# Weight conversions in five stages, and the last stage's scales, loads and splits a batch ahead on ScalarE: attention and two mixers on one core

## The chip, the cores and the metric

One core of a Trainium2 chip runs the whole program. The metric is device microseconds of one execution. The engines are named as in the profile: PE (TensorE, matrix products; PEld is its weight loads), DVE (VectorE), ACT (ScalarE), POOL (GpSimd) and SP (SyncE, whose queue issues most DMAs). Each engine works through its own queue in order; between queues there are only semaphores.

## What is computed

Causal attention of 4 batches, 12 heads, 448 positions and 64 columns per head feeds two mixers, all in float32 by the reference:

```python
scores = scale * np.matmul(q, k.transpose(0, 1, 3, 2))      # mask, softmax, then times v
x = attn_out.transpose(0, 2, 1, 3).reshape(B, S, H * D)     # 4 x 448 x 768
# first mixer
h = np.maximum(xt @ w_tok1, 0.0) @ w_tok2                   # xt: x with positions last
u = x + h.transpose(0, 2, 1)
x = u + np.maximum(u @ w_ch1, 0.0) @ w_ch2                  # 768 -> 1536 -> 768
# second mixer
theta = x @ w_theta
y = einsum(w_tok_r, x * cos(theta)) + einsum(w_tok_i, x * sin(theta))
u = x + y
out = u + np.maximum(u @ w_ch, 0.0)
```

q, k and v come as float32, the weights as float64.

## The kernel before

**Numbers.** Most products run as three fp16 matmuls (`mm3`, lines 225 to 227). A float32 tile is scaled by a power of two and *split* into a high half and a rest (`split_to`, 191): the high half is a scaled copy on ACT (L157) or POOL (L160), the rest a subtraction on DVE (L193) that reads the high half. The scale comes from `power` (133): `squares` (120) lets ACT sum a tile's squares per row (L124) into a float32 column and POOL adds a tiny constant and writes bf16 (L125); PE adds the columns over the rows with a matrix of ones (L138), DVE cuts the sum to a power of two (L140, L128), and POOL makes scale and inverse from it (L131).

**Weight conversions.** Every float64 weight tile (768 KB) is fetched as raw words (L170), ACT takes the absolute value of the high words (L173), DVE puts low bits and sign right (L180 to L182), then come squares, power and split into a `ws` tile that is stored to DRAM (384 KB) and streamed in again for each use (L220). Four tiles of the token weights and 24 of `w_ch1` and `w_ch2` are converted beside the first half of attention; the table `ROUNDINGS` says at which attention step: `round_first` (511) does the absolute values there, `round_rest` (516) everything else one step later, and then issues the fetch of the tile after next. Seven of the 24 tiles are handed to their first unit without a reload. Six tiles of `w_ch` follow late (`convert_late`).

**Stages.** (1) Attention: 4 x 6 pairs of heads x 7 tiles = 168 steps. A step's scores (L329) go through DVE (row maximum, L336) and ACT (exponential, L338); PV (L373, L384) comes `LAG` = 4 steps later. After every two pairs `tokmix` (403) mixes tokens; when a batch's three mixings are done, `split_ready` (493) computes the power of u and splits its six tiles. (2) The first mixer's channel part runs as 96 *units* (24 a batch: 6 + 6 + 6 + 6 products of 18 matmuls), the first 72 spread over attention by `UNIT_STEPS`, the first of them at step 46. They end in `x2d` in DRAM. (3) Last stage, from about 655 us: theta weights `th` and token kernel `wk` have been loaded beside the last units; for each batch the x power, six x tiles loaded from `x2d` and split, on even batches also the `rawt` tails of two batches (split into `tl`), then two halves `dh` of: theta tiles (PE, then a chain through ACT, POOL and DVE to sine and cosine products, both split), `mix` over the token kernel, and after both halves `split_u2` (814) and six output units (736). The output units of a batch run in the next one: three after its first thetas, three at its end. All splits of this stage have their high half on POOL (`split`, 706).

**Order.** The program is traced by the Python code, and a scheduler then orders each engine's queue by its own timing of the instructions; `high_priority` pulls attention forward, and `issue_after` puts what is traced inside it behind a given instruction of the same engine. So the order that the chip sees isn't the order of the code.

Of the kernel before, what the change touches and what calls it, by code (L numbers as in the profile page):

```python
# [28 lines left out]
BUFS = dict(ut=12, h2=8, acc=12, ws=8, wf=2, raw=2, sb=3, ph=3, pt=5, t=3, junk=2)  # L29
# [3 lines left out]
KEEP, UBACK = 6, 16  # L33
LATE_CONVERT = 16
FIRST_UNIT, PHASE, RATES = 46, 42, (14, 29)
UNIT_STEPS = [FIRST_UNIT + -(-n * PHASE // RATES[0]) if n < RATES[0] else
              FIRST_UNIT + PHASE + -(-(n - RATES[0]) * PHASE // RATES[1]) for n in range(72)]
AHEAD_STEPS = {0: 18, 1: 22, 2: 26, 3: 30, 4: 34, 5: 38, 12: 43, 13: 47, 14: 51, 15: 55, 16: 70, 17: 77,
               18: 80, 19: 85, 20: 88, 21: 91, 22: 94}
ROUNDINGS = sorted([(at_step, n - 4) for n, at_step in enumerate((3, 4, 8, 9))] +  # L40
                   [(AHEAD_STEPS.get(n, UNIT_STEPS[n] - 5), n) for n in range(24)])
# [15 lines left out]
def fused(ctx, tc, q, k, v, w_tok1, w_tok2, w_ch1, w_ch2, w_theta, w_tok, w_ch, out):  # L57
# [46 lines left out]
    nc.vector.memset(ones, 1.0)  # L104
    trig_k = cst.tile([P, 4], F32, tag="trig_k", name="trig_k")
# [27 lines left out]
    def power(p, s, sq):  # L133

        ps = mm_bank()
        n = sq.shape[-1]
        for j in range(n):
            nc.tensor.matmul(ps[:, 0:1], lhsT=ones, rhs=sq[:, j:j + 1], start=j == 0, stop=j == n - 1)  # L138
# [56 lines left out]
    def split_scaled(dst, f, p):  # L195
        sq = main.tile([P, 1], BF16, tag="sqb", name="sqb", bufs=4)
        s = main.tile([P, 1], F32, tag="s", name="s", bufs=4)
        squares(sq, f)
        power(p, s, sq)
        split_to("A", dst, f, s)  # L200
# [9 lines left out]
    def convert(src, kept, p):  # L210

        w, f = ws_tile(), wf_tile()
        load64(f, src, raw_tile())
        split_scaled(w, f, p)
        nc.sync.dma_start(out=kept, in_=w)
        return w
# [86 lines left out]
    class Pair:  # L303
        def __init__(self, b, pr, parts):
# [4 lines left out]
            self.pts, self.ps = {}, None  # L309
            self.native_pv = b * NPR + pr in NATPV  # L310

    def scores(pp, i, h):
# [48 lines left out]
        nc.sync.dma_start_transpose(out=pt[:, 0:nb, :], in_=ph[:, 0:nb * P])  # L361
# [154 lines left out]
    def round_rest(j):  # L516
        n, f = ROUNDINGS[j][1], rounding.pop(j)
        round64(f, fetched.pop(j)[1])
        if n < 0:
            split_w(tok_weights(n + 4)[1], f)  # L520
        else:
            w, kept = ws_tile(), jobs[n][1]
            split_scaled(w, f, jobs[n][2])
            nc.sync.dma_start(out=kept, in_=w)
            stored.add(n)
            if n not in AHEAD_STEPS:
                loaded[n] = w
        fetch(j + 2)
# [3 lines left out]
    def convert_late(n):  # L532
        while made[0] < min(n, len(late)):
            with tc.issue_after(loads[min(LATE_CONVERT, max(loads))].ins):
                convert(*late[made[0]])
            made[0] += 1

    def run_units(n):
        for _ in range(n):
# [13 lines left out]
            split_ready()  # L553
# [12 lines left out]
    def mix_tokens():  # L566
        b, g = mixes.pop()
        tokmix(b, g, xgs[b, g], xbufs, accs[b])
        split_ready()
# [14 lines left out]

    for n, (b, pr, t) in enumerate(steps):
# [9 lines left out]
        for j, (at_step, _) in enumerate(ROUNDINGS):  # L595
            if at_step == n - 1:
                with tc.issue_after(pairs[b, pr].first.ins):
                    round_rest(j)
            if at_step == n:
                with tc.issue_after(pairs[b, pr].last.ins):  # L600
                    round_first(j)
        if n >= 140:
# [17 lines left out]
    with tc.issue_after(unit_end[0].ins):  # L620
        mix_tokens()
    convert_late(len(late))
# [37 lines left out]
    power(p_wk, s_wk, sq_wk)  # L660
    for t in range(7):
        split_to("A", wk[:, t], wkf[:, t], s_wk)
# [43 lines left out]
    def split(dst, src, s):  # L706
        split_to("P", dst, src, s)
# [48 lines left out]
    trigs = {}  # L756

    for b in range(B):
        for b2 in range(b, b + 2 if b % 2 == 0 else b):
            power(p_x[:, b2:b2 + 1], s_x[:, b2:b2 + 1], sq_x[b2])  # L760
            trigs[b2] = trig_table(b2)
        raw, x2 = [], []
        for d in range(DT):
# [5 lines left out]
            raw.append(r)  # L769
            x2.append(t)  # L770
        if b % 2 == 0:
            rawt = m2.tile([P, DT, P], F32, tag="rawt", name="rawt", bufs=1)
            for d in range(DT):
                for b2 in range(2):
                    nc.sync.dma_start(out=rawt[:, d, b2 * 64:(b2 + 1) * 64], in_=x2d[b + b2][d][:, 0:64])
            tl = m2.tile([P, 2, DT, P], F16, tag="tl", name="tl", bufs=1)
            for b2 in range(2):
                c = slice(b2 * 64, (b2 + 1) * 64)
                split(tl[:, :, :, c], rawt[:, :, c], s_x[:, b + b2:b + b2 + 1])
            tail_k = m2.tile([P, 9], F32, tag="tail_k", name="tail_k", bufs=1)  # L780
            for b2 in range(2):
                r = slice(b2 * 64, (b2 + 1) * 64)
                product(tail_k[r, 0:8], trigs[b + b2][r, 0:8], 1.0, 1.0)
        mix_scale = m2.tile([P, 1], F32, tag="mix_scale", name="mix_scale", bufs=2)
        product(mix_scale, p_x[:, b:b + 1], p_wk, 2.0 ** -28)
# [17 lines left out]

        def mix(dh):
            for d in range(3):
# [101 lines left out]
```

## Time and profile before

| | us |
|---|---|
| median of 3 runs | 996.02 (994.8 to 998.42) |
| the profiled execution, its own time | 993.12 |
| its span, first to last instruction | 991.3 |
| PE busy | 889.8 |
| DVE busy | 652.4 |
| ACT busy | 493.7 |
| POOL busy | 247.9 |
| mean granted TensorE clock | 0.954 of 2.4 GHz |

The profile is one execution. A group of instructions is named by line, engine and the tiles that it writes and reads. Idle time of an engine is put down to what ended it. A matmul that was issued while the one before still ran overlaps it, so busy time of PE is counted once.

### The profile page before, as it was taken

To read this page: it belongs to the slowest core of one execution; us is meant where nothing else is said; L and a number is where in the kernel's file an instruction comes from. 1 tells how busy PE (TensorE), PEld (TensorE's weight loads), DVE (VectorE), ACT (ScalarE), POOL (GpSimd) and SP (SyncE) were. 2 spreads that over 40 slices of the span, in tenths; PEclk is the share of its full clock that TensorE was granted. 3 is DMA by queue.
4 is the path that set the end of the run, shared out by engine and by line. 5 is a ranking of instruction groups with operands and counts; after the bars stand their busy time and mean duration, and the time that the engine had idled before them with its cause. 6 is when DMAs were issued, how large, how long until landed. Compare 5 with 4: busy or idle time off the path is not lost.

```text
span 991.3 us, 16726 instructions
## 1 busy us (share of the span) xinstructions
PE 889.8 (90%) x5935; PEld 570.0 (57%) x5935; DVE 652.4 (66%) x1498; ACT 493.7 (50%) x1155; POOL 247.9 (25%) x520
## 2 busy tenths in 40 slices
PE   7988699898877999998999989949999969989998
PEld 6877577666643656665656555525555535535554
DVE  6586677958897665747776258574678555674762
ACT  6687677867675554546554246432333312321521
POOL 2121012212311010111211112263445254343240
PEclk9999899989997999998999999979999988989999
DMA  6465553647979874846576678500441130203102
GB/s 191 126 212 172 193 189 134 227 157 211 253 200 259 254 214 130 212 128 134 181 153 174 207 243 273 186 32 9 141 123 51 54 104 15 97 9 129 52 26 75
DMA packets 104788, 146.93 MB, mean 148 GB/s; under 512 B 60992, under 2 KB 72192, under 8 KB 104704
## 3 DMA queue, kind: packets, MB, share of 16 engines
q1 hardware_dynamic: 104160, 144.84, 49.9%
q0 software_dynamic: 384, 0.79, 0.3%
q8 instruction: 47, 0.77, 0.3%
q14 instruction: 37, 0.30, 0.1%
q10 hardware_dynamic: 160, 0.23, 0.1%
HBM read 109.64 MB, written 22.81 MB: 134 GB/s over the span
## 4 chain that ended last, share of the span: by engine, by line
PE 64%; DMA 11%; DVE 10%; ACT 5%; POOL 5%; issue 4%; SPq 0%; ACTq 0%; DVEq 0%; POOLq 0%
PE ps_mm L225 14%; PE ps_mm L226 14%; PE ps_mm L227 14%; DMA pt<-ph 7%; PE ps_sc L329 3%; PE ps_pv L373 3%; PE ps_mm L345 2%; PE ps_sc L225 2%; PE ps_sc L226 2%; PE ps_sc L227 2%; POOL ut L160 2%; PE ps_pv L384 1%; PE ps_mm L410 1%; PE ps_mm L411 1%; PE ps_mm L409 1%
## 5 line engine op out<-in xcount | busy, mean ns | idle before, releaser
L225 PE MATMUL ps_mm<-h,ws 128*128 128x448 f16 x432 | 155.4, 361 | 0.0
L227 PE MATMUL ps_mm<-h,ws 128*128 128x448 f16 x432 | 155.2, 360 | 0.0
L226 PE MATMUL ps_mm<-h,ws 128*128 128x448 f16 x432 | 155.1, 361 | 0.0
L225 PEld LDWEIGHTS <-ws 128*128 128x128 f16 x720 | 71.6, 99 | 71.5 <-issue 14.2
L227 PEld LDWEIGHTS <-ws 128*128 128x128 f16 x720 | 71.5, 99 | 65.4 <-issue 6.4
L225 PE MATMUL ps_mm<-ut,ws 128*128 128x448 f16 x288 | 102.7, 359 | 6.2 <-ACT ut L157 6.2
L226 PEld LDWEIGHTS <-ws 128*128 128x128 f16 x720 | 71.4, 99 | 63.7 <-issue 6.1
L226 PE MATMUL ps_mm<-ut,ws 128*128 128x448 f16 x288 | 102.3, 356 | 0.0
L227 PE MATMUL ps_mm<-ut,ws 128*128 128x448 f16 x288 | 102.2, 355 | 0.0
L338 ACT ACTIVATE sb<-sb,mx 128x192 f32<-128x192 f32 (+3 forms) x168 | 89.0, 531 | 20.1 <-DVE mx L336 19.9
L336 DVE CUSTOM_DVE_ANT_0 sb<-ps_sc,mask 128x192 f32<-128x192 f32 (+3 forms) x168 | 74.3, 456 | 19.5 <-PE ps_mm L345 12.8
L124 ACT ACTIVATE junk<-acc 128x448 bf16<-128x448 f32 x72 | 41.1, 571 | 83.9 <-DVE acc L811 44.9
L373 PE MATMUL ps_pv<-v_raw,ptf 128*128 128x128 f32 (+1 forms) x456 | 62.4, 276 | 3.8 <-ACT ptf L347 2.4
L373 PEld LDWEIGHTS ps_pv<-v_raw,ptf 128*128 128x128 f32 x456 | 58.3, 191 | 9.0 <-ACT ptf L347 3.7
L457 ACT ACTIVATE t<-ps_mm,c_scale 128x448 f32<-128x448 f32 x48 | 30.1, 626 | 58.6 <-PE ps_mm L227 41.8
L160 POOL TENSOR_SCALAR h<-t 128x448 f16<-128x448 f32 x48 | 31.9, 664 | 105.8 <-ACT t L457 105.4
L329 PE MATMUL ps_sc<-kh,qs 128*128 128x256 f32 (+2 forms) x112 | 45.1, 411 | 13.4 <-DVE mx L336 10.8
L358 DVE SCALAR_TENSOR_TENSOR ph<-sb,ph 128x64 f16<-128x64 f32 (+3 forms) x156 | 42.8, 318 | 21.5 <-ACT ph L157 20.9
L459 DVE TENSOR_TENSOR h<-t,h 128x448 f16<-128x448 f32 x48 | 30.5, 640 | 39.3 <-POOL h L160 39.2
L157 ACT ACTIVATE ph<-sb 128x192 f16<-128x192 f32 (+3 forms) x84 | 36.4, 440 | 38.9 <-DMA pt<-ph 38.3
L698 ACT ACTIVATE tmp<-tmp 128x384 f32<-128x384 f32 x28 | 14.6, 523 | 76.7 <-DVE tmp L696 76.1
L225 PE MATMUL ps_sc<-th,ut 128*128 128x384 f16 x144 | 48.9, 340 | 3.2 <-POOL ut L160 1.8
(212 smaller groups left out, 2169.8 us busy)
## 6 DMA issues: line engine op xcount, KB each, us to landing
ws<-w_c SPq DMA_DIRECT2D x113, 384.0 KB, 4.1
raw<-in_w_ch_dram SPq DMA_DIRECT2D x30, 768.0 KB, 4.8
w_c<-ws SPq DMA_DIRECT2D x30, 384.0 KB, 3.4
q_raw<-in_q_dram SPq DMA_DIRECT2D x16, 448.0 KB, 4.5
k_raw<-in_k_dram SPq DMA_DIRECT2D x16, 448.0 KB, 4.4
v_raw<-in_v_dram SPq DMA_DIRECT2D x24, 288.0 KB, 3.9
x2d<-acc SPq DMA_DIRECT2D x24, 224.0 KB, 3.2
acc<-x2d SPq DMA_DIRECT2D x24, 224.0 KB, 2.8
```

The lines of the kernel that those rows point to most:

```text
L124: nc.scalar.activation(j[:, 0:src.shape[-1]], src, AF.Square, accum_out=a)
L157: nc.scalar.activation(dst, src, AF.Copy, scale=scale)
L160: e.tensor_scalar(out=dst, in0=src, scalar1=scale, scalar2=0.0, op0=ALU.mult, op1=ALU.add)
L225: nc.tensor.matmul(ps, lhsT=ka(a[:, 0]), rhs=kb(b[:, 0]), start=first, stop=False)
L226: nc.tensor.matmul(ps, lhsT=ka(a[:, 0]), rhs=kb(b[:, 1]), start=False, stop=False)
L227: return nc.tensor.matmul(ps, lhsT=ka(a[:, 1]), rhs=kb(b[:, 0]), start=False, stop=last)
L329: nc.tensor.matmul(ps[:, 0:n], lhsT=lhs, rhs=cut(pp.kh), start=True, stop=pp.kl is None)
L336: pp.first = nc.vector.tensor_tensor_reduce(out=dst, in0=src, in1=msk, op0=ALU.add, op1=ALU.min, scale=-0.125, scalar=3.0e38, accum_out=pp ...
L338: pp.last = nc.scalar.activation(sb[:, 0:kk], sb[:, 0:kk], AF.Exp, bias=pp.mx[:, j:j + 1], scale=-1.0, accum_out=pp.sm[:, j:j + 1])
L358: nc.vector.scalar_tensor_tensor(out=dst, in0=sb[:, c0:c1], scalar=PSC, in1=hi[:, c0:c1], op0=ALU.mult, op1=ALU.subtract)
L373: pp.pv = nc.tensor.matmul(pp.ps[:, reg:reg + n], lhsT=pt[:, u], rhs=pp.v[0][:, vt * D:vt * D + n], start=(u == 0), stop=(u == len(blks) - 1))
L459: gates[0] = nc.vector.tensor_tensor(out=t[:, 1], in0=f, in1=t[:, 0], op=ALU.subtract)
```

## The change

- `squares` writes ACT's accumulator straight into the bf16 column. The POOL addition is gone; `power` starts its sum with one matmul on a constant column `tiny` instead.
- The conversions run in stages: `round_first` (absolute values) at a step, `round_bits` (DVE's bits and ACT's squares) one later, the fetch of the tile after next two later, `round_split` (power, split with the high half on POOL) three later, `round_store` five later. `round_split` is traced in `late_step`'s place, behind the PV of the step four back; fetch and store stand behind the last transposing DMA of the pair on SP. `wf` has three buffers. The steps are evenly spaced from 14 to 92. No tile is handed over: all 24 are stored and reloaded.
- Units start at step 50 and reach the old rate at 88. `split_ready` runs two steps behind a batch's last mixing (steps 48, 90, 132); for the last batch one unit later than before.
- Last stage: `split` takes ACT. The x powers of batches 0 to 2 (`x_scale`) are traced in the units of the next batch, that of batch 3 between the two mixings of batch 0; the split of `wk` moves behind the first thetas. Loads and splits of x (`load_x2`) are traced a batch ahead, before the second mixing, the tails (`load_tail`) just before; three output units come after the second thetas in place of the batch's end (two, two and two in the last batch).

```diff
-BUFS = dict(..., wf=2, ...)
+BUFS = dict(..., wf=3, ...)
+ROUND_BITS, ROUND_FETCH, ROUND_SPLIT, ROUND_STORE = 1, 2, 3, 5
...
     def squares(dst, src):
-        a = main.tile([P, 1], F32, tag="sq", name="sq", bufs=4)
-        nc.scalar.activation(j[:, 0:src.shape[-1]], src, AF.Square, accum_out=a)
-        nc.gpsimd.tensor_scalar(out=dst, in0=a, scalar1=1.0, scalar2=TINY, op0=ALU.mult, op1=ALU.add)
+            nc.scalar.activation(j[:, 0:src.shape[-1]], src, AF.Square, accum_out=dst)
...
+        nc.tensor.matmul(ps[:, 0:1], lhsT=ones, rhs=tiny, start=True, stop=False)
...
-    def round_rest(j):
+    def round_bits(j):
         round64(f, fetched.pop(j)[1])
...
+            rounding[j] = f, row_squares(f)
+    def round_split(j):
+            f, sq = rounding.pop(j)
+            rounding[j] = ws_tile()
+            split_scaled("P", rounding[j], f, jobs[n][2], sq)
+    def round_store(j):
+            nc.sync.dma_start(out=jobs[n][1], in_=rounding.pop(j))
...
+            if at[0] % 24 == 2 and 1 <= at[0] // 24 <= 3:
+                x_scale(at[0] // 24 - 1)
...
+            with tc.issue_after(pairs[steps[n - LAG][0:2]].pv.ins):
+                for j, (at_step, _) in enumerate(ROUNDINGS):
+                    if at_step == n - ROUND_SPLIT:
+                        round_split(j)
+                if n in (b2 * 42 + 48 for b2 in range(B)):
+                    split_ready()
...
     def split(dst, src, s):
-        split_to("P", dst, src, s)
+        split_to("A", dst, src, s)
...
             thetas(0)
-            run(todo, 3)
+            run(todo, n)
             mix(0)
             thetas(1)
+            run(todo, n)
+            if b < B - 1:
+                if b == 1:
+                    load_tail(2)
+                load_x2(b + 1)
             mix(1)
             f = split_u2()
-            run(todo, 3)
+            run(todo, 6 - 2 * n)
```

How this moves instructions is shown at three places. Rows are engine queues in order, with the line numbers of each kernel's own file; behind `<-` stand the tiles read.

ACT, the first converted weight tile, before (`sq` is the float32 column, `ws` the split's high half) and then after (`sqb` is the bf16 column):

```order
L347 ACTIVATE ptf<-ps_mm 128x512
L338 ACTIVATE sb_182,sm<-sb_182,mx 128x192
L173 ACTIVATE wf<-raw 128x768
L124 ACTIVATE junk,sq<-acc 128x448 x2
L124 ACTIVATE junk,sq<-wf 128x768
L157 ACTIVATE ws<-wf,s 128x768
```

```order
L340 ACTIVATE sb_186,sm<-sb_186,mx 128x320
L173 ACTIVATE wf<-raw 128x768
L349 ACTIVATE ptf<-ps_mm 128x256
L124 ACTIVATE junk,sqb<-wf 128x768
L340 ACTIVATE sb_182,sm<-sb_182,mx 128x320
L349 ACTIVATE ptf<-ps_mm 128x256
```

The high half is gone from ACT's queue, and what follows the squares is attention's next work.

The start of the last stage: POOL before (`ut<-acc` are batch 0's x splits, `tl` the tails), then ACT after, where the first unit of batch 3 is evicted by the last row:

```order
L160 TENSOR_SCALAR h_8006<-t 128x448
L131 TENSOR_SCALAR s_x<-g 128x1
L131 TENSOR_SCALAR trig<-p_x,p_th 128x1
L131 TENSOR_SCALAR s_x<-g 128x1
L131 TENSOR_SCALAR mix_scale<-p_x,p_wk 128x1
L131 TENSOR_SCALAR trig<-p_x,p_th 128x1
L131 TENSOR_SCALAR mix_scale<-p_x,p_wk 128x1
L131 TENSOR_SCALAR trig<-s_x 128x1
L160 TENSOR_SCALAR ut<-acc,s_x 128x448 x3
```

```order
L157 ACTIVATE ut<-acc,s_u 128x448 x6
L157 ACTIVATE ut<-acc,s_x 128x448
L173 ACTIVATE thf<-raw_w 128x384
L157 ACTIVATE ut<-acc,s_x 128x448 x3
L124 ACTIVATE junk,sq_x_160<-acc 128x448
L124 ACTIVATE junk,sq_th<-thf 128x768
L173 ACTIVATE thf<-raw_w 128x384 x2
L124 ACTIVATE junk,sq_th<-thf 128x768
L157 ACTIVATE tl<-rawt,s_x 128x6x64 x2
L173 ACTIVATE thf<-raw_w 128x384
L157 ACTIVATE ut<-acc,s_x 128x448
L459 ACTIVATE t<-ps_mm,c_scale_145 128x448
```

Before, the x splits stand behind the last unit's split and a row of scales; after, they stand ahead of all units of batch 3.

PE at the start of batch 2, before (the end of the powers of x, the transposes, the first theta product on the tails `tl`) and after:

```order
L138 LDWEIGHTS ones
L138 MATMUL ps_mm<-sq_x_159,ones 128x1
L712 MATMUL ps_mm<-ident,rawt 128x128 x3
L712 MATMUL ps_mm<-ident,acc 128x128 x9
L225 LDWEIGHTS tl
L225 MATMUL ps_sc<-th,tl 128x384
```

```order
L138 LDWEIGHTS ones
L138 MATMUL ps_mm<-sq_y_163,ones 128x1
L740 MATMUL ps_mm<-ident,rawt 128x128 x2
L227 LDWEIGHTS tl
L227 MATMUL ps_sc<-th,tl 128x384
```

The twelve columns of x are gone from between the batches; what stands there now is the power of batch 1's own result (`sq_y`), with one transpose of the next tails inside it.

## Rows read from the trace of the kernel before

**Rows 1.** The page: the span, then PE's busy time.

```profile
span 991.3 us, 16726 instructions
PE 889.8 (90%) x5935; PEld 570.0 (57%) x5935; DVE 652.4 (66%) x1498; ACT 493.7 (50%) x1155; POOL 247.9 (25%) x520
```

**Rows 2.** Five stages: length, then busy us of each engine, granted clock, DMA.

```profile
0.00:250.00 250.00, 216.43 (x1423) 173.32 (x1423) 180.46 (x472) 181.56 (x444) 44.40 (x117) 0.95 0.56 182
250.00:330.00 80.00, 62.30 (x491) 41.51 (x491) 65.20 (x172) 49.31 (x117) 16.39 (x35) 0.87 0.95 250
330.00:580.00 250.00, 241.72 (x1975) 155.71 (x1974) 152.17 (x402) 124.87 (x309) 33.96 (x90) 0.99 0.67 172
580.00:655.00 75.00, 70.50 (x392) 36.75 (x391) 51.41 (x120) 38.83 (x85) 18.71 (x49) 0.98 0.68 219
655.00:991.30 336.30, 298.87 (x1662) 162.70 (x1660) 203.21 (x334) 99.18 (x204) 134.41 (x231) 0.95 0.20 65
```

**Rows 3.** PE's waits, whole span: us in total, times, longest us.

```profile
PE ps_sc L225 <- POOL tl L160: 21.2, 2, 12.5
PE ps_mm L138 <- POOL sqb L125: 15.1, 8, 4.2
...
PE ps_mm L225 <- ACT ut L157: 6.2, 2, 4.5
...
PE ps_mm L225 <- POOL ut L160: 4.5, 1, 4.5
PE ps_mm L138 <- POOL sq_u L125: 4.5, 3, 1.6
...
PE ps_mm L712 <- DVE g L140: 2.0, 1, 2.0
```

**Rows 4.** Timeline 43.5 to 48.5: start, us, instruction, count, idle before.

```profile
45.81 0.83 ACT L124 ACTIVATE junk<-wf 128x768 bf16<-128x768 f32 x1
...
46.81 0.19 POOL L125 TENSOR_SCALAR sqb<-sq 128x1 bf16<-128x1 f32 x1 [0.63 <-ACT junk L124]
47.05 0.16 PE L138 MATMUL ps_mm<-sqb,ones 128*128 128x1 bf16 x1 [2.20 <-POOL sqb L125]
```

**Rows 5.** Stretches of lower granted clock: columns as in rows 2.

```profile
47.00:51.00 4.00, 3.94 (x12) 2.58 (x12) 3.71 (x12) 3.09 (x9) 0.38 (x3) 0.57 0.00 0
...
197.00:205.00 8.00, 5.87 (x22) 3.29 (x21) 6.34 (x14) 5.29 (x12) 1.20 (x4) 0.57 0.84 282
...
658.00:672.00 14.00, 3.92 (x13) 1.91 (x14) 9.72 (x13) 0.63 (x2) 11.44 (x19) 0.51 0.00 0
812.00:826.00 14.00, 6.21 (x21) 3.03 (x22) 6.53 (x9) 0.00 (x0) 9.78 (x20) 0.51 0.13 47
873.00:880.00 7.00, 5.56 (x15) 2.04 (x16) 5.81 (x11) 2.09 (x4) 3.28 (x5) 0.53 0.00 0
```

**Rows 6.** Lines L160, L193, L157: ns least, median, most; first and last start.

```profile
L160 POOL TENSOR_SCALAR h<-t x48: 562/567/1505, 131.8 to 654.7; 128x448 f16<-128x448 f32 x48
...
L160 POOL TENSOR_SCALAR h<-acc,s_y x24: 637/878/1452, 750.7 to 967.2; 128x448 f16<-128x448 f32 x24
...
L193 DVE SCALAR_TENSOR_TENSOR h<-acc,s_y,h x24: 672/1050/1057, 752.2 to 968.6; 128x448 f16<-128x448 f32 x24
...
L157 ACT ACTIVATE ut<-acc,s_u x24: 652/653/669, 120.3 to 592.6; 128x448 f16<-128x448 f32 x24
```

**Rows 7.** The chain that ended last, 895 to 912: start, us, what.

```profile
896.70 0.19 PE ps_mm L226
...
897.11 0.64 ACT t L743
...
897.78 0.80 DVE acc L744
...
898.60 2.12 DMA out_dram<-acc
...
900.74 2.47 DMA acc<-x2d
```

More of the change, by code (lines that the diff above doesn't have):

```diff
@@ L104, in fused @@
     nc.vector.memset(ones, 1.0)
+    tiny = cst.tile([P, 1], BF16, tag="tiny", name="tiny")
+    nc.vector.memset(tiny, TINY)
     trig_k = cst.tile([P, 4], F32, tag="trig_k", name="trig_k")
@@ L136, in power @@
         n = sq.shape[-1]
+        nc.tensor.matmul(ps[:, 0:1], lhsT=ones, rhs=tiny, start=True, stop=False)
         for j in range(n):
-            nc.tensor.matmul(ps[:, 0:1], lhsT=ones, rhs=sq[:, j:j + 1], start=j == 0, stop=j == n - 1)
+            nc.tensor.matmul(ps[:, 0:1], lhsT=ones, rhs=sq[:, j:j + 1], start=False, stop=j == n - 1)
         g = main.tile([P, 2], F32, tag="g", name="g", bufs=4)
@@ L568, in mix_tokens @@
         tokmix(b, g, xgs[b, g], xbufs, accs[b])
-        split_ready()
     def late_step(n):
@@ L621, in fused @@
         mix_tokens()
+    run_units(1)
+    with tc.issue_after(unit_end[0].ins):
+        split_ready()
+    run_units(1)
     convert_late(len(late))
@@ L754, in gate, with load_x2 @@
             yield
[L756 to L762, printed above, removed]
+    trigs = {b: trig_table(b) for b in range(3)}
+    x2s, raws, tails = {}, {}, {}
+    def load_x2(b):
+        x2s[b], raws[b] = [], []
         for d in range(DT):
@@ L768, in fused, with load_tail @@
                 split(t, r, s_x[:, b:b + 1])
[L769 to L776, printed above, removed]
-            for b2 in range(2):
[L778 to L785, printed above, removed]
+            raws[b].append(r)
+            x2s[b].append(t)
+    def load_tail(b):
+        rawt = m2.tile([P, DT, P], F32, tag="rawt", name="rawt", bufs=1)
+        for d in range(DT):
+            for b2 in range(2):
+                nc.sync.dma_start(out=rawt[:, d, b2 * 64:(b2 + 1) * 64], in_=x2d[b + b2][d][:, 0:64])
+        tl = m2.tile([P, 2, DT, P], F16, tag="tl", name="tl", bufs=1)
+        tail_k = m2.tile([P, 9], F32, tag="tail_k", name="tail_k", bufs=1)
+        for b2 in range(2):
+            c = slice(b2 * 64, (b2 + 1) * 64)
+            split(tl[:, :, :, c], rawt[:, :, c], s_x[:, b + b2:b + b2 + 1])
+            product(tail_k[c, 0:8], trigs[b + b2][c, 0:8], 1.0, 1.0)
+        tails[b] = tl, rawt, tail_k
+    load_tail(0)
+    load_x2(0)
+    for b in range(B):
+        raw, x2 = raws[b], x2s[b]
+        tl, rawt, tail_k = tails[b // 2 * 2]
         u2 = [None] * DT
@@ L802, in thetas @@
                 trig(trigs[b], ps_th, ps_x, put)
+        mix_scale = m2.tile([P, 1], F32, tag="mix_scale", name="mix_scale", bufs=2)
         def mix(dh):
+            if dh == 0:
+                product(mix_scale, p_x[:, b:b + 1], p_wk, 2.0 ** -28)
             for d in range(3):
@@ L824, in fused @@
             thetas(0)
+            power(p_wk, s_wk, sq_wk)
+            for t in range(7):
+                split_to("A", wk[:, t], wkf[:, t], s_wk)
             run_units(len(units) - at[0])
             thetas(1)
+            load_x2(1)
             mix(0)
+            x_scale(3)
+            trigs[3] = trig_table(3)
             mix(1)
```

64 lines of the change are left out of this document (34 added, 30 removed).

## The prediction

> **What bounds the kernel now.** I read the page's busy times first, then the same by stage, then what TensorE (PE) waited for, then the places of those waits. PE is busy 889.8 of 991.3 us [rows 1]; no other engine is near that in any stage but one (VectorE, 65.2 of 80 us between 250 and 330) [rows 2]. So time can come back only where PE stands still or runs slowly. By stage PE idles 33.6 us in 0 to 250 (attention with the weight conversions beside it), 17.7 in 250 to 330 (where the DMA queues carry a share of 0.95), 8.3 in 330 to 580, 4.5 in 580 to 655 and 37.4 in the last stage [rows 2]. The waits name the causes [rows 3]: GpSimd (POOL) ends the two longest kinds. In the first stage it is the column of squares (L125) on which the power's small matmul (L138) stands; in the last it is the split of the tails (L160). One wait of the first kind is shown step by step [rows 4]: ACT squares the converted tile (0.83), POOL adds the constant (0.19), and PE, whose queue holds the power ahead of the next transposes, has stood 2.20 us. After such a wait the granted clock is lower: 0.57 in 47 to 51 and in 197 to 205, near 0.51 at 658 to 672, 812 to 826 and 873 to 880, that is mostly the 1.2 GHz level, and 0.95 to 0.99 over most stages [rows 2, 5]. What that takes is PE's busy time in the stretch times what is missing from 1: 3.94 x 0.43 = 1.7, 5.87 x 0.43 = 2.5, 3.92 x 0.49 = 1.9, 6.21 x 0.49 = 3.0, 5.56 x 0.47 = 2.6 us [rows 5].
>
> **The change part by part.** The sums are made against the profiled execution: span 991.3, its own time 993.1; the median of the three runs is 996.0, 2.9 above it, which I add at the end.
>
> 1. *Squares without POOL.* ACT's accumulator is written as bf16, the 0.19 us addition on POOL goes, and each of 44 powers (24 conversions, 6 late ones, 4 each for u, x and y, theta, the token kernel) gets one more one-column matmul. Bounds for that: nothing, and 0.19 (a 448-column matmul of the same engine) times 44 = 8 us [rows 7]; a single column is far nearer to nothing, so I take 1 and leave it inside the rounding of the places below.
>
> 2. *Conversions in stages.* A conversion's bits are put right one tile after its absolute values, its power is traced two tiles later, behind that step's PV matmuls, and its store two tiles later still; the third `wf` tile makes that possible. So the power should find its squares done. What stands to go in 0 to 330: 15.1 (8 waits on the conversions' squares), 4.5 (3 on the mixing's), and 1.8 on ACT's split of u (6.2 less the longest, 4.5) [rows 3], 21.4 together, and the slow clock behind them: five stretches between 47 and 205, the first 1.7, the last 2.5 [rows 5], about 10. Upper end 31. Lower end: nothing or less, since PE must still wait for scores, exponentials and PV in turn, and here ACT is busy 181.6 and VectorE 180.5 of 250 [rows 2]: what PE no longer waits for at the power may be waited for one matmul later. The new order puts one to two tiles more between squares and power, not a whole pair. I take half, 15.5.
>
>  The split itself goes from ACT to POOL. POOL's split has no row of 768 columns; its 48 copies for the units have 448, a median of 0.57 and a longest of 1.5 us [rows 6], times 768/448: 1.0 to 2.6 us, and I take 1.3, nearer to the median, for VectorE is often at work beside it here. POOL is busy 44.4 of 250 [rows 2], so 24 x 1.3 = 31 fits. But VectorE's split is 0.67 alone and 1.05 beside POOL's [rows 6], so 31 us of POOL may cost VectorE up to 31 x 0.38/0.67 = 18 us; it idles 69.5 in that stretch [rows 2], so I count nothing and keep this for the rivals. The first stage's POOL queue also holds the memsets for the next pair; those wait for PE, and the splits behind them wait too.
>
>  The Trainium skill (SBUF — State Buffer, "Who interferes with whom") says that a VectorE instruction with two SBUF inputs and a GpSimd one that reads SBUF shut each other out for a whole instruction. By that, each of the 24 splits would stop VectorE for all its 1.3 us where they meet, 31 us in place of 18; the trace shows a slowing from 0.67 to 1.05, not a full stop, so the sum stays.
>
>  Seven tiles that were handed over in SBUF are now stored and loaded again: 7 loads of 384 KB, in a stretch where the DMA share is 0.56 [rows 2], two or more tiles ahead: nothing. They cost up to 4 us each if the queue had to wait for them.
>
> 3. *End of attention (near 586).* The last batch's split stands one unit later, its power's last column 14 matmuls ahead of the first user in place of 8, 6 x 0.19 = 1.1 us [rows 7]; on POOL `s_u` passes two small products. Of the 4.5 [rows 3] I take 2.
>
> 4. *Start of the last stage (655 to 668).* PE stands 12.5 us [rows 3] while POOL makes the x scales, six x splits and two tail splits one after the other, behind the units' own splits. In the changed order the x powers of batches 0 to 2 lie in the units of the next batch, and ACT makes the x and tail splits of batch 0 before it has evicted the first unit of batch 3. What is left is VectorE's second half of the x splits, six of 0.67 = 4 us, under the first theta tile, which needs only tails. 12.5 + 1.9 of clock = 14.4; a gain of more isn't there, a smaller one is if ACT or the loads are late. I take 13.
>
> 5. *Start of batch 2 (808 to 820).* The same wait takes 8.7 there (21.2 less 12.5), the power's chain 2.0 [rows 3], the clock 3.0: 13.7. The x tiles of the next batch are now loaded behind that batch's three output units and split by ACT under the second mixing. The path from the end of an output unit: eviction 0.64, addition 0.80, store 2.12, load 2.47 [rows 7], split 0.65 + 0.67 [rows 6] = 7.4 us. The mixing above it is 63 matmuls of 0.19 = 12 us, so it is covered with 4.6 to spare; without that cover the 7.4 would be paid at three batch starts. I take 12.5.
>
> 6. *Splits on ACT.* 116 splits of POOL (nine rows of its line, from 655 on; the 24 for the output units stand in [rows 6]) become ACT's, at most 0.65 each [rows 6], 75 us; ACT goes from 99 to 174 of 336 [rows 2]. VectorE's halves fall from 1.05 toward 0.67. The wait for a POOL split at 870 (4.5) with its clock (2.6) is up for gain, 7.1; ACT now also holds that tile's sines, so I take 4.
>
> Sum: 15.5 + 2 + 13 + 12.5 + 4 = 47. 993.1 - 47 = 946, and with the 2.9 **949 us**.
>
> **The rivals.**
>
> *A: the first stage gives nothing.* For it: attention there is a ring through VectorE, ACT and PE, both others busy over 70%, and POOL's splits slow VectorE. Against it: PE's queue was held by the power alone, with other work behind it. Time: 949 + 15.5 = 964.
>
> *B: ACT's queue takes the place of POOL's.* Each theta tile has two more ACT instructions in front of the next tile's, and x splits that wait for a load hold the squares behind them. For it: ACT's own waits would become PE's; against it: 174 of 336. If half of the last stage's 29.5 comes back: 949 + 15 = 964.
>
> *C: slower.* In the first stage VectorE is held by POOL and holds attention: each of 24 conversions costs its POOL split (1.3) and 0.7 of scalars and waits in front of VectorE's half, which stands in VectorE's queue ahead of the next scores: 24 x 2.0 = 48, and at POOL's long end 24 x 3.3 = 79. With parts 3 to 6 kept (31.5) and part 2 lost, all of it on the path would give 996 - 31.5 + 48 = 1012, or 1043. It decides from about 36.5 us on the path (1.5 per conversion), for 1001. Against it: VectorE's 69.5 us of idle time.
>
> *D: the change does not do what it says:* the scheduler keeps the powers behind fresh squares and the x splits late, and the time stays within 5 us of 996. The new order speaks against the second half of that at both places.
>
> **How the numbers follow.** The forecast, 925 to 960: 0.57. A and B, 960 to 976: 0.29. Both together or worse, up to 991: 0.03. D: 0.04. C: 0.05. Below 925: 0.02. The low end is everything at once: 996 - (31 + 6 + 14.4 + 13.7 + 7.1) = 924; the high end A or B with 12 more for what they take of each other. Range 925 to 976, 0.86. Half a per cent, 5 us, is about what a measurement of this kernel tells from no change: faster 0.91, same 0.04, slower 0.05.
>
> **What would show it.** In the profile after: PE's waits on the squares down from 19.6 to under 8 with the first 250 us some 15 shorter (part 2; A and C if not); no PE wait over 4 us between the last units and the first theta tile, and none over 3 at the start of batch 2, with the granted clock staying near 1 there (parts 4, 5); VectorE's splits in the last stage near 0.67 (part 6). ACT ending PE's longest waits in the last stage would be B; VectorE's first-stage splits waiting for POOL for over 1 us each, with PE waiting for the maxima, would be C. The forecast is wrong if PE's idle time only moves.

## The result and the profile after

The changed kernel takes 914.66 us (914.39 to 915.05, four runs) against 995.62 for the kernel before (994.8 to 998.42): a ratio of 0.9183 [0.9164, 0.9201], 81 us less. The forecast was 949 with a range of 925 to 976. The direction and the places were right, the size was not: 47 us were forecast.

The page of the kernel after, its span and its busy times (as rows 1):

```profile
span 913.3 us, 16742 instructions
...
PE 871.4 (95%) x5979; PEld 566.4 (62%) x5979; DVE 630.5 (69%) x1499; ACT 537.2 (59%) x1247; POOL 169.6 (19%) x313
```

The kernel after in five stretches (columns as in rows 2). The cuts lie near the ends of the stages of [rows 2], but the first does not part the same work: PE has 1600 instructions before 250 us here and 1423 there.

```profile
0.00:250.00 250.00, 230.72 (x1600) 186.34 (x1601) 206.89 (x536) 182.26 (x467) 75.72 (x116) 0.97 0.66 212
250.00:300.00 50.00, 42.67 (x357) 27.10 (x354) 44.60 (x116) 29.11 (x73) 11.84 (x21) 0.90 1.06 294
300.00:550.00 250.00, 242.35 (x1998) 156.85 (x1997) 150.18 (x402) 124.33 (x311) 28.41 (x66) 0.99 0.68 178
550.00:618.00 68.00, 66.14 (x367) 34.40 (x365) 52.20 (x120) 41.67 (x88) 23.46 (x45) 1.00 0.70 230
618.00:913.30 295.30, 289.51 (x1672) 161.73 (x1669) 176.67 (x329) 159.80 (x313) 30.16 (x66) 1.00 0.24 74
```

What had taken the first 330 us is done at about 300; the last stage went from 336.3 to 295.3, with PE idle for 5.8 in place of 37.4 and the granted clock at 1.00 in place of 0.95. The middle hardly changed: PE is busy 241.72 and 242.35 us of 250. PE's waits over the whole span (columns as in rows 3):

```profile
PE ps_pv L386 <- DMA pt<-ph: 9.6, 7, 2.7
PE ps_sc L331 <- DVE mx L338: 5.6, 6, 2.1
PE ps_sc L331 <- DMA k_pad<-in_k_dram: 4.4, 1, 4.4
PE ps_mm L227 <- DMA ws<-w_c: 4.4, 2, 3.7
...
PE ps_mm L227 <- DVE acc L845: 1.5, 1, 1.5
...
PE ps_mm L138 <- ACT junk L124: 0.6, 2, 0.3
```

The wait on squares is down from 19.6 [rows 3] to 0.6; the wait on L845 is the only one in the last stage that the trace lists. The two largest that are left belong to attention: PV behind the transposing DMAs, scores behind VectorE's maxima. Two of 4.4 us are behind loads: of k, and of stored weight tiles.

To place the gain I marked both traces by the same work: the starts of attention's exponentials 28, 56, 84 and 112 (one a step, counted from 0), the first unit of batch 3, its last unit on `w_ch1`, and the end. By these marks the kernel after is 30.7 us shorter up to step 112 (331.8 to 301.1), 5.0 shorter from there to batch 3's units, equal through these units (63.1 and 62.7), and 42.1 shorter in the last stage (337.8 to 295.7). The rows of these stretches, columns as in rows 2, before and then after:

```profile
56.70:139.90 83.20, 68.63 (x431) 55.84 (x430) 57.43 (x149) 60.32 (x147) 11.15 (x35) 0.92 0.55 190
139.90:234.40 94.50, 86.09 (x576) 66.49 (x576) 73.23 (x172) 66.93 (x156) 18.41 (x47) 0.96 0.55 184
234.40:331.70 97.30, 77.41 (x611) 52.07 (x610) 78.75 (x208) 64.41 (x152) 19.16 (x39) 0.89 0.91 244
...
653.50:991.30 337.80, 300.33 (x1688) 164.08 (x1685) 203.81 (x340) 100.21 (x205) 135.33 (x235) 0.95 0.20 65
```

```profile
59.30:128.10 68.80, 63.82 (x423) 53.22 (x422) 58.89 (x152) 54.06 (x141) 24.43 (x36) 0.95 0.69 236
128.10:212.50 84.40, 83.94 (x589) 65.36 (x587) 69.54 (x164) 57.88 (x143) 26.90 (x35) 1.00 0.63 222
212.50:301.20 88.70, 75.68 (x629) 52.67 (x627) 80.07 (x213) 58.29 (x146) 20.12 (x33) 0.90 0.92 251
...
617.60:913.30 295.70, 289.91 (x1675) 162.01 (x1673) 176.67 (x329) 160.20 (x313) 30.16 (x66) 1.00 0.24 74
```

In steps 56 to 84 (the second row of each) PE idled 8.4 us at a clock of 0.96 and now idles 0.5 at 1.00.

### The profile page after: what moved, and what is told of

Its sections match the earlier page's. It is cut to its first block, busy times and chain, and to the rows that moved or that the text cites. A ratio compares the mean times of both kernels' runs of the same rounds, so it can differ in the third digit from the quotient of the medians.

```text
span 913.3 us, 16742 instructions
## 1 busy us (share of the span) xinstructions
PE 871.4 (95%) x5979; PEld 566.4 (62%) x5979; DVE 630.5 (69%) x1499; ACT 537.2 (59%) x1247; POOL 169.6 (19%) x313
## 4 chain that ended last, share of the span: by engine, by line
PE 73%; DMA 13%; DVE 7%; ACT 4%; issue 2%; SPq 1%; POOL 0%; ACTq 0%; DVEq 0%; POOLq 0%
PE ps_mm L227 16%; PE ps_mm L228 16%; PE ps_mm L229 16%; DMA pt<-ph 6%; PE ps_pv L375 3%; PE ps_sc L227 3%; PE ps_sc L331 3%; PE ps_sc L228 3%; PE ps_sc L229 3%; DMA ws<-w_c 2%; DMA raw<-in_w_ch_dram 2%; PE ps_pv L386 2%; PE ps_mm L347 2%; PE ps_sc L333 1%; DMA rawt<-x2d 1%
## 5 line engine op out<-in xcount | busy, mean ns | idle before, releaser
L227 PE MATMUL ps_mm<-h,ws 128*128 128x448 f16 x432 | 152.6, 354 | 1.1 <-DMA ws<-w_c 0.6
L228 PE MATMUL ps_mm<-h,ws 128*128 128x448 f16 x432 | 152.8, 354 | 0.0
L229 PE MATMUL ps_mm<-h,ws 128*128 128x448 f16 x432 | 152.6, 354 | 0.0
L340 ACT ACTIVATE sb<-sb,mx 128x320 f32<-128x320 f32 (+3 forms) x168 | 89.3, 532 | 32.0 <-DVE mx L338 30.8
L338 DVE CUSTOM_DVE_ANT_0 sb<-ps_sc,mask 128x320 f32<-128x320 f32 (+3 forms) x168 | 74.3, 454 | 16.5 <-PE ps_mm L347 13.3
L375 PE MATMUL ps_pv<-v_raw,ptf 128*128 128x128 f32 (+1 forms) x456 | 65.9, 284 | 0.6 <-ACT sb L340 0.4
L375 PEld LDWEIGHTS ps_pv<-v_raw,ptf 128*128 128x128 f32 x456 | 61.7, 200 | 5.6 <-issue 1.9
L160 POOL TENSOR_SCALAR h<-t 128x448 f16<-128x448 f32 x48 | 33.1, 692 | 144.6 <-ACT t L459 144.3
L157 ACT ACTIVATE ph<-sb 128x192 f16<-128x192 f32 (+3 forms) x84 | 36.0, 441 | 37.4 <-DMA pt<-ph 36.8
L130 POOL TENSOR_SCALAR f<-p_w,c_h 128x1 f32<-128x1 f32 x48 | 22.9, 479 | 145.1 <-DVE acc L473 129.0
L331 PE MATMUL ps_sc<-k_pad,q_raw 128*128 128x192 f32 (+3 forms) x112 | 41.1, 467 | 8.0 <-DMA k_pad<-in_k_dram 4.4
```

The costliest lines, as they stand in the source:

```text
L157: nc.scalar.activation(dst, src, AF.Copy, scale=scale)
L160: e.tensor_scalar(out=dst, in0=src, scalar1=scale, scalar2=0.0, op0=ALU.mult, op1=ALU.add)
L227: nc.tensor.matmul(ps, lhsT=ka(a[:, 0]), rhs=kb(b[:, 0]), start=first, stop=False)
L228: nc.tensor.matmul(ps, lhsT=ka(a[:, 0]), rhs=kb(b[:, 1]), start=False, stop=False)
L229: return nc.tensor.matmul(ps, lhsT=ka(a[:, 1]), rhs=kb(b[:, 0]), start=False, stop=last)
L331: nc.tensor.matmul(ps[:, 0:n], lhsT=lhs, rhs=cut(pp.kh), start=True, stop=pp.kl is None)
```

## The experiments

All ratios are to the kernel before. The five questions come in the order in which they arose.

**Do the two ends of the program add up?** `first_only` is the changed kernel with the old last stage, `last_only` the old kernel with the new last stage.

> The changed kernel with the last stage of the kernel before (scales, loads, splits on POOL as they were): the staged conversions, the direct squares, the later batch splits alone. Theory 1, the two halves of the change add up: the changed kernel's gains up to the last stage stay, 30.7 us to step 112 and 5 to the first unit of batch 3, so 995.6 - 36 = 960 us (956 to 964). Rival, they need each other (the x powers in the units, what the scheduler orders across the border): 970 or more.

> The kernel before with the changed last stage alone (x powers in the units, x loads and splits a batch ahead on ACT, the token kernel's split behind the first thetas). Theory 1, the halves add up: 995.6 - 42 = 954 us (950 to 958), with PE idle in the last stage near the 5.8 us of the changed kernel. Rival, part of the 42 came with the direct squares or the better end of attention: 962 or more.

Measured: `first_only` 955.45, 0.9593 [0.9536, 0.965]; `last_only` 954.48, 0.9583 [0.9529, 0.9636]. The gains are 4.1% and 4.2%, some 40.5 and 41.5 us; their sum is the whole, within intervals of about half a per cent on either side. So neither end was seen to feed the other, and the forecast was short at both: 17.5 for parts 2 and 3 together, 29.5 for parts 4 to 6.

**In the last stage: the engine of the splits, or the order?**

```diff
 # after_pool_splits, on the changed kernel
-        split_to("A", dst, src, s)
+        split_to("P", dst, src, s)
 # before_act_splits, on the kernel before
-        split_to("P", dst, src, s)
+        split_to("A", dst, src, s)
```

> The changed kernel with the high halves of the last stage's splits put back on POOL, everything else as changed. Theory 'order': the 42 us of the last stage came from x work that is traced early and a batch ahead; POOL has the room (about 134 of 295 us), so the time stays at 915 to 925. Theory 'engine': POOL's slow splits, and VectorE's slowed beside them (1.05 for 0.67), were the cause: at least half of the 42 comes back, 936 or more.

> The kernel before with one word changed: the last stage's splits on ACT. Theory 'order': the waits of 12.5 and 8.7 us at the two starts remain up to what a faster split takes off (6 x 0.2 and VectorE's 8 x 0.35 at each), so 985 to 992 us. Theory 'engine': most of the 42 is gained by this alone, 965 or less.

Measured: `after_pool_splits` 921.36, 0.9247 [0.9172, 0.9321]; `before_act_splits` 977.08, 0.9811 [0.9754, 0.9868]. In the new order the engine is worth about 7 us: the two ratios differ by 6.4 us, and their intervals would allow anything from nothing to 14, but by the marks the last stage of `after_pool_splits` is 303.0 us for 295.7. Part 6 had 7.1 up for gain, of which I took 4. In the old order the same word is worth about 19, largely because ACT shortens the very row of splits that PE waits for at both batch starts. PE's longest wait there in `before_act_splits`, whose last stage by the marks was 318.5 us (337.8 in the kernel before):

```profile
PE ps_sc L225 <- ACT tl L157: 10.6, 2, 7.5
```

The wait for the tails is 10.6 there, 21.2 in the kernel before [rows 3], and 0 with the new order. Order and engine overlap; order is the larger part (35 of 42 by `after_pool_splits`). Which of the order's moves gave how much (the powers in the units, the loads a batch ahead, the output units in another place) was not tried.

**In the first stage: the delay, the engine of the conversions' split, or the squares?**

```diff
 # after_no_delay
-ROUND_BITS, ROUND_FETCH, ROUND_SPLIT, ROUND_STORE = 1, 2, 3, 5
+ROUND_BITS, ROUND_FETCH, ROUND_SPLIT, ROUND_STORE = 1, 2, 1, 2
 # after_front_power: the same, and the power traced right behind the bits
+                    round_split(j)          # behind round_bits(j)
 # after_act_conv
-            split_scaled("P", rounding[j], f, jobs[n][2], sq)
+            split_scaled("A", rounding[j], f, jobs[n][2], sq)
 # after_pool_squares: squares() and power() as before (POOL's addition,
 # no matmul on the constant column)
```

> The changed kernel with the two waiting steps taken out of the conversions: power and split are traced one step after the absolute values, with the bits and squares, and the store one step later (1, 2, 1, 2 in place of 1, 2, 3, 5). Theory 'delay': PE stood still because the power stands in its queue ahead of fresh squares; then PE's waits on the squares come back and most of the first stage's 31 us with them, 935 to 946 us. Rival 'relief': the gain came from what ACT and POOL no longer do (high halves off ACT, additions off POOL) and from even spacing: 914 to 922.

> The changed kernel with power and split traced in the place of the kernel before: one step after the absolute values, together with the bits, behind the row maximum of the step's scores in place of the PV matmuls of the step four back; store one step later. Theory 'place' (PV's place, not the two tiles of delay, kept PE from meeting fresh squares): PE's waits on squares return between steps 28 and 56, where 14 us were gained, so 922 to 930. Rival 'spacing plus direct squares': within 5 us of the 910 to 915 of the changed kernel.

> The changed kernel with the high halves of the 24 converted tiles on ACT again. Theory 'relief' (ACT, busy 182 of 250 us, was the ring's slow part): 24 x 0.93 = 22 us of ACT come back, and with them up to 20 us of time, 925 to 936. Theory 'delay': PE's queue was the cause, ACT has room, and DVE is no longer slowed by POOL: within 5 us of 914.7.

> The changed kernel with the old squares: ACT sums into float32, POOL adds the constant and writes bf16 (0.19 us each, 115 of them), no extra matmul. With the delay of two steps there is room for POOL's 0.19: within 5 us of 914.7 by the theory 'delay'. If the hop over POOL itself was what PE waited for, or POOL's queue (now with 24 splits of 768 columns in it) holds the additions back: 925 or more.

Measured: `after_no_delay` 910.38, 0.9147 [0.9099, 0.9195]; `after_front_power` 911.25, 0.9163 [0.9113, 0.9213]; `after_act_conv` 913.17, 0.9158 [0.911, 0.9205]; `after_pool_squares` 928.27, 0.9325 [0.9293, 0.9358]. Taking the delay out of the changed kernel costs nothing, nor does giving the split back to ACT: my theory that the gain needs the delay fell here. Only the squares' form counts, 14 us, and by the marks 6.1 of them lie before step 112 (307.2 for 301.1). But these kernels have both the new squares and the new steps, so two edits were tried in the kernel before, alone and together:

```diff
 # before_direct_squares: squares() and power() of the change
 # before_even
+AHEAD_STEPS = {n: 14 + n * 78 // 23 for n in range(24)}
 # before_even_direct: both
 # before_even_late
+AHEAD_STEPS = {n: 14 + n * 66 // 18 if n < 19 else 85 + (n - 19) * 3 for n in range(24)}
```

> The kernel before with the direct squares alone (ACT's accumulator as bf16, one more small matmul in each power). If the hop over POOL is worth what its return cost in the changed kernel (13.6 us): 981 us (977 to 985). If it matters only in the new order: 990 to 997.

> The kernel before with the changed kernel's steps for the 24 conversions (evenly from 14 to 92, all stored and reloaded) and nothing else. Theory 'spacing' (the dense steps 59 to 80 of before overload ACT and VectorE, and the late ones fall into the stage full of DMA): 10 us or more of the first stage's 31 are gained, 985 or less. Theory 'delay': the powers still stand ahead of fresh squares, 990 to 997.

> The kernel before with two parts: the changed kernel's even steps for the 24 conversions, and the direct squares. Theory 'spacing plus direct squares': 995.0 - 22.5 - 13.6 = 959 us, so nearly the 955.5 of the changed first stage, and neither the stages of a conversion nor the later batch splits are needed. Rival: they matter too, 966 or more.

> As the run of before with even steps, but the last five conversions at before's own steps 85, 88, 91, 94, 97, in the stage whose DMA share is 0.9, and the first nineteen evenly from 14 to 80. Theory 'late ones' (two conversions less in the transposes' stage gave the 10 us between steps 95 and 112): 980 to 986. Theory 'density' (the dense steps 59 to 80 were it): 970 to 975 as with even steps to 92.

Measured: `before_direct_squares` 962.62, 0.9683 [0.9626, 0.9741]; `before_even` 972.54, 0.9781 [0.9734, 0.9828]; both, 958.74, 0.9656 [0.9603, 0.9709]; `before_even_late` 977.99, 0.9839 [0.9791, 0.9887]. The direct squares, which I had priced at nothing, give 31 us alone, and with the even steps 34, nearly all of the first stage's 40. The two overlap: 31 and 22 don't make 34. By the marks, `before_even_late` has steps 84 to 112 at 96.2 us like the kernel before (97.3), where `before_even` has 84.7: that stretch, with a DMA share of 0.91 above, pays for the two more conversions put there. Steps 56 to 84 are 81.0 us in `before_even` and 80.1 in `before_even_late`, from 94.5: that is the wider spacing.

**Why is a POOL addition of 0.19 us worth 31?** Three guesses: the hop between engines, the missing delay, the operation. `before_reload` parts the even steps from the reload that came with them.

```diff
 # before_act_squares
-        nc.gpsimd.tensor_scalar(out=dst, in0=a, scalar1=1.0, scalar2=TINY, op0=ALU.mult, op1=ALU.add)
+        nc.scalar.activation(dst, a, AF.Copy, bias=TINY, scale=1.0)
 # before_power_late: a conversion's power, split and store one step later
+            if at_step == n - 2:
+                with tc.issue_after(pairs[b, pr].first.ins):
+                    round_late(j)
 # before_reload
-            if n not in AHEAD_STEPS:
-                loaded[n] = w
```

> The kernel before, with the constant added by ACT right behind its own squares, in place of POOL. The operation stays (one more ACT instruction for each column, 0.2 us), the hop to another engine goes. If what the direct squares gave (962.6 in place of 993.5) was the time that the column spends between two engines and in POOL's queue, most of it is here too: 962 to 972. If it was the operation itself, or PE's queue in another order for any reason, the time is 985 or more.

> The kernel before, POOL's addition kept, but a conversion's power, split and store traced one attention tile later than its bits and squares. This is the delay of the change alone, in the order that has the hop. The prediction's theory (PE waits because the power is traced too close behind the squares) expects most of the gain of the direct squares: 962 to 975. The theory that the hop has to go, whatever the delay, goes by the changed kernel with POOL's addition, where three tiles of delay left 14 of the 31 us in place: 975 to 985.

> The kernel before with its own steps, but no tile handed over: all 24 are stored and loaded again. It parts the even steps (972.5, with the reload in it) from the reload. Even steps alone: 990 to 998 here. If the reload freed something (a ws buffer that a handed tile holds for five steps): below 985.

Measured: `before_act_squares` 999.19, 1.0056 [1.0028, 1.0085]; `before_power_late` 985.51, 0.9911 [0.9881, 0.9941]; `before_reload` 1001.65, 1.0085 [1.0051, 1.0119]. The hop was not it: without it the time did not fall, and PE now waited for ACT's addition (19.9 us, 11 times). One step of delay gives a third at most. And the reload costs 8 us by itself, which I had put at nothing; its trace has a wait that the kernel before does not have, of PE for reloaded weight tiles, between steps 56 and 84:

```profile
PE ps_mm L225 <- DMA ws<-w_c: 5.7, 2, 5.5
```

So the even steps, tried with the reload, are worth nearer 30 than 22, if the two add up.

Then PE's queue was read, in the kernel before and in `before_direct_squares`. The matmul on the constant column takes the place that the power had; the matmul on the squares stands several rows further back. Two kernels part that matmul from POOL's instruction:

```diff
 # before_pool_tiny: POOL's addition stays
+        nc.tensor.matmul(ps[:, 0:1], lhsT=ones, rhs=tiny, start=True, stop=False)
 # before_direct_no_tiny: squares() of the change, power() as before
```

> The kernel before, POOL's addition and its hop kept, and only the one-column matmul on the constant column put in front of each power. In PE's queue that matmul takes the place that the power had, and the matmul on the squares moves several rows back: the first stand behind 57, 60, 87 and 87 PV matmuls in place of 53, 57, 76 and 84, as with the direct squares. If PE's order is what the direct squares gave: 962 to 972. If it was POOL's instruction: 994 to 1000.

> The kernel before with the direct squares, without POOL's addition, and without the matmul on the constant column (the constant is left out of the sum). PE's order is then nearly that of before (the first powers behind 53, 57, 76 and 84 PV matmuls). If PE's order is what counts: 985 to 995, the hop's 0.3 us for each of 24 at most. If POOL's instruction was what cost: 960 to 970.

Measured: `before_pool_tiny` 965.45, 0.9678 [0.9642, 0.9714]; `before_direct_no_tiny` 979.2, 0.9811 [0.9775, 0.9846]. One more matmul, with POOL's addition left where it was, gives all that the direct squares gave (0.9683). Here are PE's queue around the first conversion in the kernel before, and in `before_pool_tiny` (`ident` rows are transposes, `ps_pv` PV):

```
L345 MATMUL ps_mm<-ident,sb_182 128x128 x4
L227 MATMUL ps_mm<-wt2_179,h1_511 128x448
L227 MATMUL ps_mm<-wt2_179,h1_511 128x448
L329 MATMUL ps_sc<-k_pad,q_raw 128x320
L373 MATMUL ps_pv<-v_raw,ptf 128x128 x4
L138 LDWEIGHTS ones
L138 MATMUL ps_mm<-sqb,ones 128x1
```

```
L139 LDWEIGHTS ones
L139 MATMUL ps_mm<-tiny,ones 128x1
L332 MATMUL ps_sc<-k_pad,q_raw 128x320
L348 MATMUL ps_mm<-ident,sb_186 128x128 x4
L376 MATMUL ps_pv<-v_raw,ptf 128x128 x4
L348 MATMUL ps_mm<-ident,sb_182 128x128
L348 MATMUL ps_mm<-ident,sb_184 128x128 x2
L332 MATMUL ps_sc<-k_pad,q_raw 128x448 x2
L376 MATMUL ps_pv<-v_raw,ptf 128x128 x4
...
L141 MATMUL ps_mm<-sqb,ones 128x1
```

And on the chip, the same conversion in `before_pool_tiny`; [rows 4] are its counterpart:

```profile
46.57 0.83 ACT L126 ACTIVATE junk<-wf 128x768 bf16<-128x768 f32 x1
...
46.83 1.05 PE L376 MATMUL ps_pv<-v_raw,ptf 128*128 128x128 f32 x8
...
47.94 0.39 PE L332 MATMUL ps_sc<-k_pad,q_raw 128*128 128x128 f32 x2
...
48.81 0.19 POOL L127 TENSOR_SCALAR sqb<-sq 128x1 bf16<-128x1 f32 x1
...
49.05 0.16 PE L141 MATMUL ps_mm<-sqb,ones 128*128 128x1 bf16 x1
```

POOL's addition ends at 49.00 here, 1.5 us behind ACT's read of the sum, later than in [rows 4], and PE loses nothing: ten matmuls run between the squares and the power, and no idle time stands in its row. PE's waits to 330 us in `before_pool_tiny`, then in `before_direct_no_tiny`:

```profile
PE ps_pv L387 <- DMA pt<-ph: 8.4, 3, 3.8
...
PE ps_mm L141 <- POOL sq_u L127: 3.3, 2, 2.5
...
PE ps_mm L141 <- POOL sqb L127: 1.7, 3, 0.8
```

```profile
PE ps_mm L137 <- ACT junk L124: 19.1, 10, 4.3
```

The wait on squares is 5.0 us in the first (with the mixing's, `sq_u`) and 19.1 in the second, for 19.6 in the kernel before. Up to step 84 these waits account for nearly all that differs between kernels that differ only in how a power is made and placed:

| up to step 84, us | length | PE idle | of it on squares | PE busy | clock |
|---|---|---|---|---|---|
| `before_act_squares` | 235.5 | 32.6 | 19.7 | 202.9 | 0.94 |
| the kernel before | 234.5 | 31.4 | 18.2 | 203.1 | 0.95 |
| `before_direct_no_tiny` | 229.2 | 26.4 | 12.6 | 202.8 | 0.96 |
| `before_power_late` | 224.4 | 24.5 | 12.1 | 199.9 | 0.95 |
| `before_pool_tiny` | 209.7 | 17.0 | 5.0 | 192.7 | 0.98 |
| `before_direct_squares` | 206.3 | 14.3 | 2.7 | 192.0 | 0.99 |

The longer PE waits on squares, the longer the stretch; PE's other idle time stays between 11.6 and 13.8 us, and with 1313 to 1317 matmuls in each its busy time is some 10 us shorter in the two with the constant column, at the higher clock. The rows of the kernel before and of `before_pool_tiny` (columns as in rows 2):

```profile
0.00:234.50 234.50, 203.12 (x1313) 163.76 (x1314) 167.94 (x438) 167.59 (x411) 41.72 (x113) 0.95 0.55 180
```

```profile
0.00:209.70 209.70, 192.69 (x1315) 156.92 (x1316) 164.34 (x429) 164.89 (x408) 47.24 (x109) 0.98 0.61 198
```

One gain does not fit. `before_direct_no_tiny`, 18 us faster than the kernel before by its median, has half of that in steps 84 to 112 (88.4 for 97.3), where PE waits 6.5 us on squares in place of 1.4. What became shorter there are the waits for VectorE's maxima (7.5 to 3.0) and for the transposing DMAs (7.3 to 1.5). Why is open, and whether the scheduler's other changes in a kernel play a part was not tried.

**Is there more in the first stage?** `after_front_early` is `after_front_power` with the conversions from step 12 to 81.

```diff
-ROUNDINGS = [...] + [(14 + n * 78 // 23, n) for n in range(24)]
+ROUNDINGS = [...] + [(12 + n * 69 // 23, n) for n in range(24)]
```

> The changed kernel without the delay and with the power in its old place (911.3), and its conversions three in nine steps as before but closer, from step 12 to 81 in place of 14 to 92, so that none lies in steps 84 to 112, where PE still idles 7 to 13 us and the DMA share is 0.9. If conversions there cost what the even steps suggest: 903 to 909. If the idle time there belongs to the transposes alone, or if denser conversions cost as much before step 84: 910 to 918.

Measured: 910.83, 0.9166 [0.9133, 0.9199]. Against `after_front_power`, from which it differs by its steps alone, steps 84 to 112 fell from 90.5 to 85.1 us, but steps 28 to 84 rose from 160.3 to 162.7, and what follows step 112 by 4.7. (In the kernel after, with the delay, the two stretches are 88.7 and 153.2.) The gain moved and came to nothing; no version was shown to beat the changed kernel.

## Why the prediction was wrong in size and right in kind

**Part 1, priced at nothing: the step that failed most.** I took 1 us for 44 new matmuls and missed what they do to the queue. In the old kernel that matmul alone is worth 31 us (`before_pool_tiny`): the matmul on the squares then stands several rows further back, and up to step 84 PE waits 5.0 us on squares in place of 18.2 and is busy 10.4 us less for the same work at a higher clock. POOL's 0.19 us were not the cost (`before_act_squares`): POOL's name at the end of the wait [rows 3, 4] told who was last, and PE's position told why it hurt. An operation on the path of a wait was costed by its duration; it should have been looked for in the queue's order, row by row.

**Part 2: right mechanism, halved without need.** I put 31 us up for grabs (21.4 of waits, 10 of clock) and took half, expecting PE to wait one matmul later. Measured to step 112: 30.7, of which 24.6 is idle time (51.3 to 26.7) and the rest is PE's shorter busy time at a higher clock. The discount had no row behind it. Putting it down to the delay was wrong in this sense: with the constant column there, the delay is worth nothing (`after_no_delay`). The delay without the column is in `after_pool_squares`, beside the even steps: PE waits 3.5 us on squares there, and the time to step 112 is 24.6 us below the kernel before. So either puts work between squares and power, and one of them is nearly enough. The delay in the old steps was tried for one step only (`before_power_late`). The even steps, a part of the change that stands in no term of the sum, give 22 us alone in the old kernel.

**Part 2, POOL's splits.** The 24 splits took 0.91 us in the median, but 10 of them took longer, up to 1.75, and the mean is 1.14: 27 us of POOL for the 31 forecast.

```profile
L160 POOL TENSOR_SCALAR ws<-wf,s x24: 905/907/1747, 42.0 to 278.0; 128x768 f16<-128x768 f32 x24
```

```profile
L193 DVE SCALAR_TENSOR_TENSOR ws<-wf,s,ws x24: 969/1012/1299, 43.9 to 279.1; 128x768 f16<-128x768 f32 x24
```

VectorE's half has a median of 1.012 (1.014 in the kernel before). That tells nothing of POOL's influence: it reads POOL's copy and starts behind it, and only 3 of the 24 ran beside another copy of POOL. What VectorE does beside these splits is other work, above all the bits of the next tiles (`wf<-raw,wf`, 0.95 us alone). Two such meetings:

```profile
72.82 1.62 POOL L160 TENSOR_SCALAR ws<-wf,s 128x768 f16<-128x768 f32 x1
220.99 0.91 POOL L160 TENSOR_SCALAR ws<-wf,s 128x768 f16<-128x768 f32 x1
```

```profile
72.71 0.96 DVE L181 SCALAR_TENSOR_TENSOR wf<-raw,wf 128x768 uint32<-128x768 uint32 x1
221.09 1.62 DVE L182 SCALAR_TENSOR_TENSOR wf<-raw,wf 128x768 uint32<-128x768 uint32 x1
```

The one that started first took its usual time, the other some 0.7 us more, that is, most of what the two shared. The trace has 83 overlaps of 0.3 us or more in which a VectorE instruction with two SBUF inputs had begun first: in the median it took 0.01 us more than usual, and POOL's instruction 0.44 of the 0.56 us shared. The rule that I cited from the Trainium skill (SBUF — State Buffer, "Who interferes with whom"), by which the two engines shut each other out, is borne out by these rows more nearly than the prediction allowed when it read 0.67 to 1.05 as a mere slowing. It cost no time that the runs show, since `after_act_conv`, without these splits on POOL, is equal within its interval.

**Part 2, the reload, priced at nothing:** `before_reload` shows 8 us in the old order, and 5.7 us of waits for reloaded tiles. The change has the reload and is faster all the same; a wait of the same kind takes 4.4 us in it.

**Part 3:** 2 forecast. The stretch from step 112 to batch 3's first unit, in which the wait of 4.5 lay, is 5.0 us shorter, and no wait of PE for ACT's split of u is left in it. So this came whole too; `first_only`, with the same code there, still shows 2.7 of it, so it isn't safe.

**Parts 4 to 6: places right, all discounts wrong.** 29.5 forecast, bounds of 35.2, measured 42.1. Idle time fell by 31.7 (37.5 to 5.8) where the named waits made 27.7; PE's busy time fell by 10.4 (300.33 to 289.91) where the clock terms made 7.5. The rest I take to be small waits and short stretches of low clock that I had not listed; they were not added up one by one. The path of 7.4 us for the x tiles was covered, as reckoned, and VectorE's halves are as forecast:

```profile
L193 DVE SCALAR_TENSOR_TENSOR ut<-acc,s_x,ut x24: 671/680/925, 619.4 to 821.4; 128x448 f16<-128x448 f32 x24
L193 DVE SCALAR_TENSOR_TENSOR h<-acc,s_y,h x24: 675/676/683, 697.6 to 890.8; 128x448 f16<-128x448 f32 x24
```

In `after_pool_splits` the second of these has a median of 1.05 again, as in [rows 6].

**The rivals.** A: no, the first stage gave 40. B: no, no wait of PE for ACT is listed in the last stage, though ACT is busy 159.8 of 295.3 us. C: no; VectorE waited 4.7 us in all for POOL's conversion splits, 0.8 at the longest. D: no. The range failed at its low end, for which everything had to come at once: 72.2 us, and I gave 2 in 100 to anything beyond. By the marks 77.8 came. (The 6 in that sum for part 3 has no row; part 3 itself names 4.5.)

## What to carry to other kernels

When an in-order engine waits for a small result, look at what stands between producer and consumer in that engine's queue before looking at the producer: here one more cheap matmul, which moved the consumer back by several rows, gave 31 us, while moving the producer's last step to another engine gave nothing and a delay of one step in the code gave 9. Where a scheduler sets the order, any added or removed instruction can move its neighbours, so read the queue and cost the new places, not only the instruction. And waits that were named, large and had independent work queued behind them went whole here, together with low clock behind them; a discount needs a row that says what will be late next.

## What was not expected of the hardware

- Where a VectorE instruction with two inputs in SBUF and a POOL copy overlapped, the one that began first kept its time and the other took longer by most of the overlap: POOL's split of 768 columns 1.62 us for 0.91 behind VectorE, VectorE's `wf<-raw,wf` 1.62 for 0.95 behind POOL. In the old last stage, where POOL's next copy runs beside VectorE's half, that half of 448 columns takes 1.05 for 0.68 [rows 6].
- A [128 x 1] addition takes as long on ACT, in the median 0.20 us, as on POOL (0.19, [rows 4]); moved to ACT, right behind the squares, it made the kernel no faster (999.2 against 994.0).
- In the last stage of the kernel after, in which PE idles 5.8 of 295.3 us, the granted clock is 1.00, the 2.4 GHz level; in the kernel before, with 37.4 us idle, it was 0.95, and near 0.51 behind the long waits [rows 5].
